# One over the deviation from Ln and Exp alone in an attention-with-norm kernel, with one activation table from the start and a new order of its first twelve blocks

## The chip, the cores and the metric

The kernel runs on one core of one Trainium2 chip. The core has five engines with queues of their own: TensorE (PE, with its weight loads shown apart as PEld), VectorE (DVE), ScalarE (ACT), GpSimd (POOL) and SyncE (SP, which here only issues DMAs). The metric is the device time of one execution in microseconds (us), taken as a median over several runs. The kernel before has a median of 792.28 us over 3 runs (791.06 to 794.29).

## The reference, cut to what matters

```python
x = A_x                                    # [1, 2048, 640] bf16
xn = (x - mean(x)) / sqrt(var(x) + 1e-5)   # per row of 640
# A: 32 heads of 192, the last 512 of 2048 cached keys and values
q = (xn @ wq).reshape(1, 2048, 32, 192).transpose(0, 2, 1, 3)
p = softmax(q @ k[:, :, -512:].T * 192 ** -0.5)
s = (p @ v[:, :, -512:]) -> [1, 2048, 6144] @ wo
# B: r = xn @ w_r; the two rows with the largest r get a gated MLP added
g = silu(B(xn))
out = x + s * g
```

What this case is about is the second line, and the order in which the first part of A is worked through.

## The kernel before, in words

Everything is one program for one core. The 2048 rows are 16 tiles of 128 (`n` = 0 to 15) in four quarters of four tiles (`t5` = 0 to 3). The 32 heads are 8 groups of 4, that is 2 pairs per group. A step `i` is one group, one quarter and one pair (64 steps); it has two blocks `b` (128 blocks in all), and each block two halves `a` of one row tile each. The order of every engine's queue is written out by hand: an instruction stands in its engine's queue where the Python emits it. The first 12 blocks (the head) come from the string `FIRST` (L618 to L636), whose tokens are worked off by `first` (L538); blocks 12 to 125 follow the fixed list `BLOCK` (L962); the last two follow `LAST`.

The tokens of the head that the change and the prediction speak of:

- `lx`, `lk`, `lq`, `x`, `k`, `v`, `wq`, `wo`: DMAs of x, keys, values and weights, most of them on SP's queue. `ko` orders the keys on POOL (L119), `kT` turns them by a DMA (L123), `kturn` turns the first pair's keys on PE.
- `bn.n.c` and `st.t5.i`: statistics of a row tile on DVE (L247 and L505, closed by L249 and L507). `sa` does the same for some tiles of the last quarter on ACT (L516, L520).
- `dev.n` (L252, ACT) and `app.n` (L255 and L256, DVE): deviation and normalisation of the four tiles of the first quarter. `nw.t5.i` (L217 to L240 and L188) is one over the deviation of the other quarters, in seven instructions per quarter, and `ap.n.e` (L181) their normalisation on the engine `e` (`a` ACT, `v` DVE, `g` POOL).
- `turn.n.e`: five PE transposes of a normalised tile (L274) and the copy into `xnT` on ACT or DVE (L275).
- `exp`: an explicit load of the activation table (L560).
- `q.i.c.e`: one third of the queries of a step (`q_whole`, L300, five matmuls; with a fourth number, for half of the rows) and their scaling into `qT` on DVE (L304) or ACT (L306). `qa` and `qb` are the same in two phases of half-height matmuls (L331, L341).
- `S.b.a`: scores of a half block (L358, six matmuls). `M.b.a`: its row maximum on DVE (L363). `E.b.a`: two exponentials on ACT (L370) and, with `.s` or at the second half, the DMA transpose of the result into `pT`.
- `P.b.e`: products with the values (L401), one over the sum on DVE (L408), and the scaling of the two halves on the two engines named: DVE (L412, one instruction) or ACT (L415, two instructions). `W.k`: products with `wo` (L443).

Scores live in two PSUM buffers (`ps_s`): `S` of a half block needs the `E` of the half block two places before it. Four smaller PSUM buffers (`ps_f`) serve `turn`, `q`, `P` and `W` in the head. `M` of a half block has to be done before its `E`. In this way PE, DVE and ACT pass each half block around, and each engine works strictly in the order of its queue.

Of the kernel before, what the change touches and what calls it, by code (L numbers as in the profile page):

```python
# [21 lines left out]
def kernel(ctx, tc, A_x, A_k_cache, A_v_cache, A_wq, A_wo, B_x, B_w_r, B_w_gate, B_w_up, B_w_down, out):  # L22
# [157 lines left out]

    def ln_apply(eng, n, src):  # L181
        if eng == "a":
            nc.scalar.activation(out=xn[:, n, :], in_=src, func=ACT.Identity, bias=nmr[:, n:n + 1], scale=rstd[:, n:n + 1])
# [4 lines left out]
    def ln_nmr(mean_ap, rstd_ap, nmr_ap):  # L188
        nc.vector.scalar_tensor_tensor(out=nmr_ap, in0=mean_ap, scalar=-1.0, in1=rstd_ap, op0=ALU.mult, op1=ALU.mult)
# [27 lines left out]
    def rsqrt_parts(var_ap, out_ap):  # L217

        T = {}

        def ln():
            T["v"] = small.tile([P, 4], FP32, name="nw_v")
            T["a"] = small.tile([P, 4], FP32, name="nw_a")
            nc.scalar.activation(out=T["a"], in_=var_ap, func=ACT.Ln, bias=eps_t[:, 0:1], scale=1.0)

        def ex():
            nc.scalar.activation(out=out_ap, in_=T["a"], func=ACT.Exp, scale=-0.5)

        def v():
            nc.gpsimd.tensor_scalar(out=T["v"], in0=var_ap, scalar1=EPS, scalar2=None, op0=ALU.add)  # L230

        def s1():
            nc.vector.scalar_tensor_tensor(out=T["a"], in0=out_ap, scalar=-0.5, in1=out_ap, op0=ALU.mult, op1=ALU.mult)

        def s2():
            nc.vector.tensor_tensor(out=T["a"], in0=T["a"], in1=T["v"], op=ALU.mult)

        def s3():
            nc.vector.scalar_tensor_tensor(out=out_ap, in0=T["a"], scalar=1.5, in1=out_ap, op0=ALU.add, op1=ALU.mult)
# [10 lines left out]

    def first_dev(n):
        nc.scalar.activation(out=rstd[:, n:n + 1], in_=mv[:, n, 1:2], func=ACT.Sqrt, bias=eps_t[:, 0:1], scale=1.0)  # L252

    def first_apply(n):
        nc.vector.reciprocal(out=rstd[:, n:n + 1], in_=rstd[:, n:n + 1])  # L255
        nc.vector.tensor_scalar(out=xn[:, n, :], in0=x_in[0][:, n, :], scalar1=mv[:, n, 0:1], scalar2=rstd[:, n:n + 1],  # L256
                                op0=ALU.subtract, op1=ALU.mult)
# [13 lines left out]
    def turn_tile(n, copy):  # L271
        tp = f_tile([P, DC, P], BF16, "tp")
        for dc in range(DC):
            nc.tensor.transpose(out=tp[:, dc, :], in_=xn[:, n, dc * P:(dc + 1) * P], identity=ident)  # L274
        copy(out=xnT[:, n], in_=tp)  # L275

# [84 lines left out]
    def row_max(b, a):  # L361
        nm_of[b, a] = small.tile([P, 2], FP32, name="nm")
        rm = nc.vector.tensor_reduce(out=nm_of[b, a], in_=s_of[b, a], axis=AX.X, op=ALU.max, negate=True)  # L363
# [690 lines left out]
```

## Time and profile before

| | before |
|---|---|
| median of 3 runs | 792.28 us |
| the profiled execution | 792.27 us |
| its span, first to last instruction | 790.3 us |
| TensorE's granted clock | 1.0 |
| busy: PE, DVE, ACT, POOL | 776.1, 580.0, 526.5, 339.6 us |
| the head (to the first matmul of block 12) | 84.06 us |

The times of the profile count from the span's start. The profiled execution lies 1.97 us above its span and 0.01 us from the median. A row of a group of instructions has the line of the kernel, the engine, the operation, what it writes and reads, how often it ran, its busy time, the mean of one in ns, and the idle time of the engine just before it with what ended that. The table of stretches has a row for each stretch of the span with the busy time of each engine in it. The chain of waits starts from the last instruction and goes back, at each step to what released it.

### The profile page before, as it was taken

The page shows a single profiled execution, that of the slowest core. Times are in us where ns is not written, and L with a number is a line of the kernel's source. Part 1 is how long each engine was busy: PE and PEld are TensorE (multiplying, and loading weights), DVE is VectorE, ACT ScalarE, POOL GpSimd, SP SyncE. Part 2 cuts the span into 40 slices and gives each one's busy share as a digit, 9 for nine tenths or more (in the row PEclk, how much of TensorE's full clock was granted, in tenths as well). Part 3 has the DMA queues.
Part 4 walks back from the last instruction along what each step waited for, and adds up shares of the span by engine and source line. Part 5 has one row for each costly group of instructions (what it writes and reads, how often), then busy time and mean ns, then how long its engine had stood idle before and what let it go on. Part 6 is the DMA issues. An engine that isn't in the chain of part 4 may idle for free.

```text
span 790.3 us, 27041 instructions
## 1 busy us (share of the span) xinstructions
PE 776.1 (98%) x11380; PEld 572.6 (72%) x11380; DVE 580.0 (73%) x1073; ACT 526.5 (67%) x950; POOL 339.6 (43%) x282
## 2 busy tenths in 40 slices
PE   8899999999999999999999999999999999999997
PEld 4457677777777777777777777777777777777775
DVE  7898788887787767667766766766766776776775
ACT  6676666677666677777666666766666666666661
POOL 1334110023110226626210102569986894266895
PEclk9999999999999999999999999999999999999999
DMA  9989999899999999999999999999999899999993
GB/s 240 196 170 174 174 184 170 146 193 163 175 187 188 211 176 192 191 170 201 175 200 183 194 218 183 158 191 188 165 176 179 149 187 168 182 179 169 181 177 93
DMA packets 447418, 142.18 MB, mean 180 GB/s; under 512 B 414724, under 2 KB 446726, under 8 KB 447296
## 3 DMA queue, kind: packets, MB, share of 16 engines
q1 hardware_dynamic: 437456, 130.84, 99.9%
q10 hardware_dynamic: 8816, 6.76, 3.2%
q0 software_dynamic: 1024, 2.85, 1.4%
q8 instruction: 89, 1.46, 0.8%
q14 instruction: 33, 0.27, 0.1%
HBM read 40.31 MB, written 2.63 MB: 54 GB/s over the span
## 4 chain that ended last, share of the span: by engine, by line
PE 90%; DVE 3%; DMA 3%; ACT 2%; issue 1%; POOL 1%; POOLq 0%; SPq 0%; DVEq 0%; ACTq 0%
PE w L443 25%; PE q_ps L331 24%; PE o_ps L401 20%; PE s L358 19%; DVE nm L363 1%; PE q_ps L300 1%; ACT pexp L370 1%; DMA pT<-pexp 1%; DMA v_sb<-in_A_v_cache_dram 1%; DMA out_dram<-fin_o 1%; DMA oT<-o_sb 0%; ACT xnT L275 0%; POOL fin_o L487 0%; DMA x_in<-in_A_x_dram 0%; PE tp L274 0%
## 5 line engine op out<-in xcount | busy, mean ns | idle before, releaser
L363 DVE TENSOR_REDUCE nm<-s 128x2 f32<-128x1024 f32 x256 | 313.0, 1223 | 137.7 <-PE s L358 135.8
L370 ACT ACTIVATE pexp<-s,nm 128x512 bf16<-128x512 f32 x512 | 324.1, 688 | 97.2 <-DVE nm L363 91.4
L331 PE MATMUL q_ps<-xnT,wq_g 64*128 64x512 bf16 (+1 forms) x2340 | 232.5, 323 | 0.0
L443 PE MATMUL w<-wo_g,oT 64*128 64x320 bf16 (+1 forms) x3096 | 231.4, 295 | 0.1
L358 PE MATMUL s<-kT,qT 64*128 64x512 bf16 x1536 | 211.5, 376 | 2.8 <-ACT pexp L370 2.6
L443 PEld LDWEIGHTS <-oT 64*128 64x128 bf16 x3096 | 170.1, 94 | 58.5 <-DMA oT<-o_sb 0.9
L401 PEld LDWEIGHTS <-pT 64*128 64x128 bf16 x4096 | 177.3, 94 | 31.4 <-issue 2.8
L401 PE MATMUL o_ps<-v_sb,pT 64*128 64x193 bf16 x4096 | 195.4, 243 | 2.9 <-DMA pT<-pexp 2.0
L415 ACT ACTIVATE o_sb<-o_ps,rl 128x192 bf16<-128x192 f32 x246 | 90.1, 418 | 128.8 <-DVE rl L408 128.5
L331 PEld LDWEIGHTS <-wq_g 64*128 64x128 bf16 x2340 | 125.7, 99 | 46.0 <-DVE qT L304 0.5
L149 POOL COPY wo_g<-wo_g 64x1920 bf16<-64x1920 bf16 x32 | 57.3, 1793 | 187.9 <-DMA wo_g<-in_A_wo_dram 165.5
L358 PEld LDWEIGHTS <-qT 64*128 64x128 bf16 x1536 | 84.7, 94 | 58.0 <-issue 3.8
L482 DVE TENSOR_TENSOR s_acc<-s_acc,w 128x320 f32<-128x320 f32 x192 | 85.0, 484 | 31.3 <-PE w L443 31.2
L343 ACT ACTIVATE qT<-q_ps 128x1024 bf16<-128x1024 f32 x114 | 92.4, 811 | 7.1 <-PE q_ps L331 1.0
L412 DVE TENSOR_TENSOR o_sb<-o_ps,rl 128x384 bf16<-128x384 f32 x133 | 74.1, 557 | 4.7
L119 POOL COPY k_perm<-k_raw 128x768 bf16<-128x768 bf16 x30 | 24.3, 826 | 94.1 <-DMA k_raw<-in_A_k_cache_dram 69.7
L893 POOL TENSOR_SCALAR yh<-y_bc,oh 128x640 f32<-128x640 f32 x32 | 60.3, 1884 | 4.7 <-DMA y_bc<-y_d 1.9
L894 POOL TENSOR_TENSOR xn<-xn,yh 128x640 bf16<-128x640 bf16 x32 | 45.0, 1406 | 2.7
L880 POOL TENSOR_TENSOR tz<-tz,xn 128x640 f32<-128x640 f32 x16 | 22.4, 1399 | 54.4 <-ACT tz L879 54.4
L408 DVE RECIPROCAL rl<-o_ps 128x2 f32<-128x2 f32 x256 | 30.7, 160 | 13.6 <-PE o_ps L401 8.9
L953 POOL TENSOR_TENSOR s_acc<-s_acc,x_fin 128x640 f32<-128x640 f32 x16 | 22.4, 1398 | 11.3 <-DMA x_fin<-in_A_x_dram 10.5
L881 POOL TENSOR_TENSOR xn<-tz,xn 128x640 bf16<-128x640 f32 x16 | 22.4, 1398 | 1.3
(140 smaller groups left out, 274.9 us busy)
## 6 DMA issues: line engine op xcount, KB each, us to landing
wo_g<-in_A_wo_dram SPq DMA_DIRECT2D x32, 240.0 KB, 4.1
k_raw<-in_A_k_cache_dram SPq DMA_DIRECT2D x32, 192.0 KB, 3.3
v_sb<-in_A_v_cache_dram SPq DMA_DIRECT2D x32, 192.0 KB, 3.8
wq_g<-in_A_wq_dram SPq DMA_DIRECT2D x14, 288.0 KB, 3.8
pT<-pexp SPq DMA_TRANSPOSE x246, 4.0
wq_g<-in_A_wq_dram SPq DMA_DIRECT2D x14, 192.0 KB, 3.4
x_fin<-in_A_x_dram SPq DMA_DIRECT2D x16, 160.0 KB, 3.8
oT<-o_sb SPq DMA_TRANSPOSE x126, 3.6
```

What stands on the lines that cost most here:

```text
L149: nc.gpsimd.tensor_copy(out=grp[g][("wo", pr)][half(1), cs, :], in_=grp[g][("wo", pr)][half(0), cs, :])
L331: mm = nc.tensor.matmul(q_ps[k][:, 0:n] if type(q_ps) is list else q_ps[:, k, 0:n], lhsT=wq[half(r), dc, c:2 * Dh:3], rhs=xnT[half(r), tok ...
L343: nc.scalar.activation(out=out, in_=q_ps[:, :, 0:n], func=ACT.Copy, scale=scale)
L358: nc.tensor.matmul(s_of[b, a][:, r, :], lhsT=qT_of[i][half(r), c, u * P:(u + 1) * P], rhs=grp[g][("kT", pr)][half(r), :, c, :], start=(c = ...
L363: rm = nc.vector.tensor_reduce(out=nm_of[b, a], in_=s_of[b, a], axis=AX.X, op=ALU.max, negate=True)
L370: nc.scalar.activation(out=p_ring[:, b % 2, a, :, hh, :].rearrange("p (x j) e -> p x j e", x=2), in_=s_of[b, a][:, hh, :].rearrange("p (j ...
L401: nc.tensor.matmul(o_of[b][r][:, a, 0:Dh + 1], lhsT=pT_ring[half(r), b % RP, a, k, :], rhs=v_ring[half(r), (g * PAIRS + pr) % RV, k, 0:Dh ...
L412: nc.vector.tensor_tensor(out=o_sb, in0=src, in1=rl[:, r].unsqueeze(2).unsqueeze(3).to_broadcast([P, 2, 3, HK]), op=ALU.mult)
L415: nc.scalar.activation(out=o_sb[:, a], in_=src[:, a], func=ACT.Copy, scale=rl[:, r, a:a + 1])
L443: nc.tensor.matmul(w_ps[r][:, 0:cs.stop - cs.start], lhsT=oT_ring[half(r), bs[pr] % RT, c, :], rhs=grp[g][("wo", pr)][half(r), c, cs], sta ...
L482: nc.vector.tensor_tensor(out=acc, in0=acc, in1=src, op=ALU.add)
L893: nc.gpsimd.tensor_scalar(out=yh, in0=M["y_bc"][:, j, :], scalar1=M["oh"][:, n, j:j + 1], scalar2=None, op0=ALU.mult)
```

## The change

One over the deviation is now made by the same two ACT instructions for all tiles: `Ln` of the variance plus epsilon, then `Exp` with a scale of -0.5 (`ln_rstd`). In the first quarter they stand for the `Sqrt` on ACT and the reciprocal on DVE; in the other quarters, where `Ln` and `Exp` were there already, the three instructions of the Newton step on DVE, the added epsilon on POOL and the shifted mean `nmr` on DVE are gone. The normalisation is now (x - mean) * rstd everywhere (`ln_rows`), no longer x * rstd + nmr. The explicit load of the table that has both functions stands on ACT's queue right after its two first DMA issues, ahead of all work, and no other table is loaded in the head. The string `FIRST` has a new order, in which some instructions also change their engine. A new token `tt.n` (`turn_pair`) turns two row tiles at once by twenty transposes of half height, which end in two copies. `q_phase` and the scaling are made more general; what they emit for the tokens used is as before. The two gathered rows of part B lose their shifted mean in the same way; their own Newton steps stay.

```diff
-    def ln_apply(eng, n, src):
-        if eng == "a":
-            nc.scalar.activation(out=xn[:, n, :], in_=src, func=ACT.Identity, bias=nmr[:, n:n + 1], scale=rstd[:, n:n + 1])
-            return
-        (nc.gpsimd if eng == "g" else nc.vector).tensor_scalar(
-            out=xn[:, n, :], in0=src, scalar1=rstd[:, n:n + 1], scalar2=nmr[:, n:n + 1], op0=ALU.mult, op1=ALU.add)
-
-    def ln_nmr(mean_ap, rstd_ap, nmr_ap):
-        nc.vector.scalar_tensor_tensor(out=nmr_ap, in0=mean_ap, scalar=-1.0, in1=rstd_ap, op0=ALU.mult, op1=ALU.mult)
+    def ln_rstd(out, var):
+        t = small.tile([P, 4], FP32, name="ln_v")[:, 0:out.shape[-1]]
+        nc.scalar.activation(out=t, in_=var, func=ACT.Ln, bias=eps_t[:, 0:1], scale=1.0)
+        nc.scalar.activation(out=out, in_=t, func=ACT.Exp, scale=-0.5)
+
+    def ln_rows(eng, out, src, mean, r):
+        (nc.gpsimd if eng == "g" else nc.vector).tensor_scalar(out=out, in0=src, scalar1=mean, scalar2=r, op0=ALU.subtract, op1=ALU.mult)
+
+    def ln_apply(eng, n, src):
+        ln_rows(eng, xn[:, n, :], src, mv[:, n, 0:1], rstd[:, n:n + 1])
...
-    def rsqrt_parts(var_ap, out_ap):
...
-        return [ln, ex, v, s1, s2, s3]
...
+    def first_apply(n):
+        ln_apply("v", n, x_in[0][:, n, :])
+
     def first_dev(n):
-        nc.scalar.activation(out=rstd[:, n:n + 1], in_=mv[:, n, 1:2], func=ACT.Sqrt, bias=eps_t[:, 0:1], scale=1.0)
-
-    def first_apply(n):
-        nc.vector.reciprocal(out=rstd[:, n:n + 1], in_=rstd[:, n:n + 1])
-        nc.vector.tensor_scalar(out=xn[:, n, :], in0=x_in[0][:, n, :], scalar1=mv[:, n, 0:1], scalar2=rstd[:, n:n + 1],
-                                op0=ALU.subtract, op1=ALU.mult)
+        ln_rstd(rstd[:, n:n + 1], mv[:, n, 1:2])
...
+    def turn_pair(n, es):
+        tp = [f_tile([P, 2, DC, P // 2], BF16, "tp") for _ in range(2)]
+        for u in range(2):
+            for dc in range(DC):
+                for r in range(2):
+                    nc.tensor.transpose(out=tp[r][:, u, dc, :], in_=xn[half(r), n + u, dc * P:(dc + 1) * P], identity=ident[half(r), half(r)])
+        for r in range(2):
+            copies[es[r]](out=xnT[:, n:n + 2, :, half(r)], in_=tp[r])
...
     FIRST = """
-    lx.0.s lx.1.a lk.0.s lk.1.s lq.0.a lx.2.s lx.3.s v.0 x.1.0 bn.0.0 bn.1.0 x.1.1 bn.1.1 dev.1 bn.0.1 app.1 dev.0 k.1.0 app.0 bn.2.0 turn.0.a bn.3.0 bn.3.1 turn.1.a v.1 kturn.av bn.2.1 wq.1 dev.3 q.0.2.0.a k.1.1 q.0.0.0.v dev.2 v.2 q.0.1.0.a
-    ko.1 app.2 app.3 st.1.0
-    S.0.0 M.0.0 exp x.2 turn.2.a turn.3.a S.0.1 kT.1 M.0.1 st.1.1 E.0.0.s st.1.2 wo.0 q.0.1.1.a q.0.0.1.a q.0.2.1.v E.0.1
-    S.1.0 wo.1 st.1.3 st.1.4 S.1.1 M.1.0 st.1.5 E.1.0.s q.1.1.a M.1.1 q.1.2.a E.1.1 st.1.6 q.1.0.v st.1.7 nw.1.0
-    S.2.0 nw.1.1 nw.1.2 M.2.0 wo.2 S.2.1 nw.1.3 nw.1.4 nw.1.5 M.2.1 nw.1.6 st.2.0 E.2.0.s ap.7.g ap.6.v P.0.vv E.2.1
-    S.3.0 M.3.0 ap.4.a v.3 S.3.1 turn.6.a ap.5.g wd.0 turn.5.a turn.4.v turn.7.v E.3.0.s st.2.1 st.2.2 P.1.va M.3.1 wo.3 st.2.3 E.3.1 q.2.1.a q.2.2.v st.2.4 wd.1 q.2.0.v P.2.va
-    S.4.0 M.4.0 S.4.1 E.4.0 x.3 M.4.1 st.2.5 q.3.1.a E.4.1 wd.2 st.2.6 st.2.7 nw.2.0 q.3.2.a nw.2.1 nw.2.2
-    S.5.0 M.5.0 nw.2.3 E.5.0 nw.2.4 q.3.0.v S.5.1 wd.3 nw.2.5 sa.3.0.0 nw.2.6 M.5.1 E.5.1 sa.3.2.0 W.0.v ap.10.g
-    S.6.0 ap.11.g M.6.0 gk.0 E.6.0 ap.9.g ap.8.v W.1.v P.3.av S.6.1 M.6.1 P.4.va
-    S.7.0 st.3.6 E.6.1 turn.10.v turn.11.v turn.9.a turn.8.v sa.3.0.1 M.7.0 S.7.1 E.7.0 gk.1 q.4.2.v gq.0 q.4.1.v q.4.0.a
-    qa.5.0.1 sa.3.1.0
-    S.8.0 M.7.1 go.0 E.7.1 st.3.7 gw.0 sa.3.2.1 sa.3.1.1 nw.3.0 nw.3.1 M.8.0 W.2.v qb.5.0.1 nw.3.2 nw.3.3 nw.3.4 nw.3.5 P.5.av S.8.1 M.8.1 gq.1 nw.3.6 E.8.0 E.8.1 P.6.va ap.15.v
-    qa.5.2 ap.12.v
-    S.9.0 S.9.1 M.9.0 ap.14.g turn.12.v turn.14.v E.9.0 ap.13.g qb.5.2 turn.13.v M.9.1 turn.15.v
-    S.10.0 gT.0 E.9.1 gk.2 gk.3 P.7.vv W.3.v M.10.0 E.10.0 S.10.1 gv.0 P.8.vv W.4.a
-    qa.6.0.1 M.10.1 gd.0
-    S.11.0 E.10.1 M.11.0 B.11 go.1 E.11.0 W.5.v qb.6.0.1 P.9.av q.6.2.v S.11.1 M.11.1 E.11.1 gw.1 gv.1
+    lx.0.s lx.1.a lk.0.s lk.1.s lq.0.a exp lx.2.s lx.3.s v.0 x.1.0 bn.1.0 bn.0.0 bn.1.1 x.1.1 bn.0.1 dev.1 dev.0 wq.1 app.1 app.0 bn.2.0 turn.1.a turn.0.a k.1.0 bn.3.0 k.1.1 kturn.av ko.1 v.1 v.2 bn.3.1 bn.2.1 q.0.2.0.a dev.3 dev.2 q.0.0.0.v app.2 st.1.0 app.3 q.0.1.0.a x.2 kT.1
+    S.0.0 M.0.0 turn.2.a turn.3.a st.1.1 S.0.1 E.0.0.s q.0.1.1.a M.0.1 q.0.0.1.a q.0.2.1.a E.0.1
+    S.1.0 st.1.2 q.1.2.a st.1.3 S.1.1 st.1.4 M.1.0 E.1.0 M.1.1 st.1.5 wo.0 wo.1 E.1.1 q.1.1.a wo.2 st.1.6 q.1.0.v st.1.7
+    S.2.0 M.2.0 S.2.1 nw.1.0 st.2.0 E.2.0.s M.2.1 ap.6.v P.0.va S.3.0 M.3.0 ap.7.g wd.0 v.3 ap.4.v E.2.1 tt.6.va
+    S.3.1 ap.5.g turn.5.a E.3.0.s turn.4.v st.2.1 st.2.2 P.1.av st.2.3 M.3.1 q.2.2.a q.2.1.v E.3.1 q.2.0.v st.2.4 wo.3 P.2.va
+    S.4.0 S.4.1 M.4.0 wd.1 E.4.0 x.3 M.4.1 E.4.1 q.3.1.a st.2.5 st.2.6 wd.2 q.3.2.a S.5.0 M.5.0 E.5.0.s q.3.0.v st.2.7
+    S.5.1 M.5.1 nw.2.0 wd.3 sa.3.0.0 E.5.1 W.0.v ap.11.g S.6.0 M.6.0 P.3.va ap.9.g ap.10.g sa.3.2.0
+    S.6.1 M.6.1 ap.8.v W.1.v E.6.0 P.4.va E.6.1 gk.0 gk.1 st.3.6 S.7.0 turn.9.v turn.11.v turn.8.a turn.10.v M.7.0
+    S.7.1 q.4.0.a gq.0 M.7.1 gw.0 E.7.0 sa.3.0.1 gq.1 q.4.1.a q.4.2.v sa.3.1.0 st.3.7 qa.5.0.1
+    S.8.0 E.7.1 sa.3.1.1 sa.3.2.1 nw.3.0 go.0 M.8.0 W.2.v qb.5.0.1 P.5.av S.8.1 M.8.1 E.8.0.s E.8.1 P.6.va qa.5.2 ap.14.g ap.12.v
+    S.9.0 S.9.1 ap.15.g M.9.0 ap.13.g turn.14.v turn.12.v E.9.0.s qb.5.2 M.9.1 gT.0 gv.0 turn.13.v turn.15.a
+    S.10.0 M.10.0 gk.2 P.7.va W.3.v E.9.1 E.10.0 W.4.a P.8.vv S.10.1 gk.3 qa.6.0.1 go.1 M.10.1
+    S.11.0 M.11.0 gd.0 E.10.1 W.5.v qb.6.0.1 E.11.0 P.9.va B.11 q.6.2.a S.11.1 M.11.1 E.11.1 gv.1 gw.1
     """.split()
...
-            M["rs2"] = M["s"].tile([2, 2], FP32, name="rs2")
+            M["rs2"] = M["s"].tile([2, 1], FP32, name="rs2")
...
-            ln_nmr(mv2[:, 0:1], rs2[:, 0:1], rs2[:, 1:2])
-            nc.vector.tensor_scalar(out=M["xsel"][0:2, :], in0=M["xg"], scalar1=rs2[:, 0:1], scalar2=rs2[:, 1:2], op0=ALU.mult, op1=ALU.add)
+            ln_rows("v", M["xsel"][0:2, :], M["xg"], mv2[:, 0:1], rs2)
```

More of the change, by code (lines that the diff above doesn't have):

```diff
@@ L215, in rsqrt_newton @@
         return [one, two, three] + [s1, s2, s3] * 3
-    def rsqrt_parts(var_ap, out_ap):
[L219 to L239, printed above, removed]
-        return [ln, ex, v, s1, s2, s3]
     st0 = {}
@@ L340, in q_phase @@
                 for k in range(2):
-                    nc.scalar.activation(out=out[:, k], in_=q_ps[k][:, 0:n], func=ACT.Copy, scale=scale)
+                    q_scale(es[k], out[:, k], q_ps[k][:, 0:n])
             else:
-                nc.scalar.activation(out=out, in_=q_ps[:, :, 0:n], func=ACT.Copy, scale=scale)
+                q_scale("a", out, q_ps[:, :, 0:n])
     s_of = {}
```

44 lines of the change are left out of this document (28 added, 16 removed).

## The prediction, made before the changed kernel ran

> **What bounds the kernel now.** I read the page first, then the chain of waits, then a table of stretches cut where the chain changes hands.
>
> ```profile
> span 790.3 us, 27041 instructions
> PE 90%; DVE 3%; DMA 3%; ACT 2%; issue 1%; POOL 1%; POOLq 0%; SPq 0%; DVEq 0%; ACTq 0%
> ```
>
> ```profile
> 10.60:23.00 12.40, 10.78 (x83) 5.21 (x84) 11.20 (x23) 9.74 (x19) 1.89 (x3) 1.00 1.12 234
> 23.00:36.10 13.10, 10.78 (x142) 6.91 (x140) 11.67 (x27) 8.28 (x14) 7.02 (x5) 1.00 1.07 188
> 36.10:52.70 16.60, 16.13 (x198) 9.89 (x194) 15.95 (x34) 12.36 (x27) 5.38 (x9) 1.00 0.82 170
> 52.70:66.10 13.40, 13.28 (x159) 8.17 (x160) 10.35 (x23) 11.28 (x25) 3.96 (x10) 1.00 0.96 160
> 66.10:84.06 17.96, 17.93 (x253) 12.95 (x252) 13.62 (x26) 10.00 (x20) 6.61 (x13) 1.00 1.06 180
> 84.06:780.00 695.94, 694.10 (x10416) 521.13 (x10416) 505.50 (x908) 469.40 (x838) 308.40 (x230) 1.00 1.07 180
> ```
>
> Behind the stretch's bounds and its length stand the busy us of PE, PEld, DVE, ACT and POOL, then PE's granted clock and the DMA share. From 84.06 on, PE is busy 694.10 of 695.94 us and the other engines have room. The same holds from 66.10. The change leaves that work as it is, apart from two tiny instructions of part B. So the time is 84.06, the end of the head, plus a rest of 792.27 - 84.06 = 708.2 us that I hold fixed. A microsecond gained or lost in the head is one in the result if it is still there at 66.1. All that PE does not work between 10.6 and 66.1 is 1.62 + 2.32 + 0.47 + 0.12 = 4.5 us. Its rows also stretch where it is fed late, so a little more can be had.
>
> ```profile
> 11.05 1.28 ACT L560
> 12.34 1.29 ACT xnT L275 x2
> ...
> 30.55 4.30 DMA v_sb<-in_A_v_cache_dram
> ...
> 42.26 1.16 DVE nw_a L233
> ...
> 52.67 0.82 PE s L358 x6
> 53.50 3.35 PE q_ps L300 x15
> ...
> 63.70 1.08 ACT pexp L370 x2
> ...
> 66.07 0.82 PE s L358 x6
> ```
>
> These are pieces of the chain, start, length, engine and line. Before 52.67 it runs mostly through DVE and ACT, at 52.67 it passes to PE, from 63.70 to 66.03 to ACT once more, and from 66.07 it is PE alone. The change touches three of these pieces by name: the table load, a Newton instruction (L233), and the late load of the values, which in the new order stands ahead of the DMA transpose of E.2.1.
>
> **The change part by part.** The durations are means of the same forms, over the head:
>
> ```profile
> L370 ACT ACTIVATE pexp<-s,nm 128x512 bf16<-128x512 f32 x46 | 29.1, 688 | 12.6 <-DVE nm L363 9.3 <-PE o_ps L401 3.2
> L401 PE MATMUL o_ps<-v_sb,pT 64*128 64x193 bf16 x320 | 16.0, 243 | 1.2 <-DVE xnT L275 0.6 <-DMA v_sb<-in_A_v_cache_dram 0.4 <-DMA pT<-pexp 0.2
> L412 DVE TENSOR_TENSOR o_sb<-o_ps,rl 128x384 bf16<-128x384 f32 x13 | 7.2, 557 | 0.5
> L274 PE MATMUL tp<-ident,xn 128*128 128x128 bf16 x80 | 5.6, 220 | 1.1 <-DVE xn L256 1.1
> L415 ACT ACTIVATE o_sb<-o_ps,rl 128x192 bf16<-128x192 f32 x14 | 5.1, 419 | 4.4 <-DVE rl L408 4.4
> L306 ACT ACTIVATE qT<-q_ps 128x512 bf16<-128x512 f32 x6 | 3.5, 601 | 1.5 <-PE q_ps L300 1.5
> L520 ACT ACTIVATE xn<-x_in,sums 128x640 bf16<-128x640 bf16 x3 | 2.5, 841 | 0.0
> L256 DVE TENSOR_SCALAR xn<-x_in,mv,rstd 128x640 bf16<-128x640 bf16 x4 | 1.8, 446 | 0.1
> L252 ACT ACTIVATE rstd<-mv,eps_t 128x1 f32<-128x1 f32 x4 | 1.2, 300 | 3.0 <-DVE mv L249 2.7 <-DVE rstd L255 0.3
> L183 ACT ACTIVATE xn<-x_in,nmr,rstd 128x640 bf16<-128x640 bf16 x1 | 0.9, 917 | 0.0
> L224 ACT ACTIVATE nw_a<-mv,eps_t 128x4 f32<-128x4 f32 x3 | 0.9, 305 | 1.0 <-DVE mv L507 0.6 <-POOL mv L521 0.3
> L227 ACT ACTIVATE rstd<-nw_a 128x4 f32<-128x4 f32 x3 | 0.6, 213 | 0.1
> L255 DVE RECIPROCAL rstd<-rstd 128x1 f32<-128x1 f32 x4 | 0.6, 146 | 0.1
> L236 DVE TENSOR_TENSOR nw_a<-nw_a,nw_v 128x4 f32<-128x4 f32 x3 | 0.5, 163 | 0.3
> L189 DVE SCALAR_TENSOR_TENSOR nmr<-mv,rstd 128x4 f32<-128x4 f32 x3 | 0.5, 154 | 0.0
> ```
>
> The first four tiles: Sqrt (0.300) becomes Ln and Exp (0.305 + 0.213), 0.22 us more per tile on ACT; the reciprocal (0.146) leaves DVE. Tiles 0 and 1 lose nothing, since DVE has the other tile's statistics to do meanwhile. For tiles 2 and 3 all four ACT instructions stand in a row ahead of the scaling of a query third, so the last normalisation comes up to 2 x 0.22 = 0.44 later.
>
> The table: the Sqrt table's load at the start is replaced one for one, and the one at 11.05 goes. What it held up are the copies at 12.34. But those need transposes that ran only just then:
>
> ```profile
> 11.62 0.73 PE L274 MATMUL tp<-ident,xn 128*128 128x128 bf16 x10
> ```
>
> Five of these ten are done about 0.37 after their start, at 12.0. So of the 1.28 us at most 0.34 lay on the path, the rest beside these transposes. With 0.44 against it, the bounds to 23.0 are a gain of 0.34 and a loss of 0.44, and I take nothing.
>
> The Trainium skill, "ScalarE: Activation LUTs", section "What ACT_TABLE_LOAD costs", gives a switch as about 1.28 us of load and 1.38 us of drain. By that the removal would free 2.66 us of ACT, and if all of the drain counted the time would be 1.4 us less than mine. The trace agrees on the load and shows no drain: the load ends at 12.33 and the copy starts at 12.34.
>
> The Newton step and the shifted mean: four DVE instructions per quarter, two of them at 0.163 and 0.154 and two of the same size and kind, 4 x 0.158 = 0.63 us. From 23.0 to 36.1 DVE loses this and half of P.0's scaling (0.557), and gains ap.4 (0.446; the new subtract form is the one of L256): 0.74 less on an engine busy 11.67 of 13.10. ACT gains two scalings (0.84) and loses ap.4 (0.917). On the other side, P.0's scalings now stand on ACT ahead of E.2.1, which has to free the buffer for S.3.1. That makes S.3.1 about a microsecond late, but its row maximum was queued on DVE until long after it:
>
> ```profile
> 26.70 0.82 PE L358 MATMUL s<-kT,qT 64*128 64x512 bf16 x6 [0.84 <-ACT pexp L370]
> ...
> 31.76 1.21 DVE L363 TENSOR_REDUCE nm<-s 128x2 f32<-128x1024 f32 x1
> ```
>
> S.3.1 ended at 27.52 and waited 4.2 us for DVE, which hides it. Bounds here: 0.74 and the 0.4 that PE waited for the values, 1.1 gained, to 0.84 lost if the scaling on ACT holds the exponentials after all. DVE is the busier engine, so I take 0.5 gained. The paired transposes of tiles 6 and 7 are not in the trace: 20 at 16.0/320 = 0.05 (the half-height products with the values) are 1.0 us, against 10 x 0.07 = 0.7 before, with 0.35 (two side by side) and 1.4 (each at the full price) as bounds; PE has 2.3 us free here, so this costs nothing, and up to 0.7 if it had none.
>
> From 36.1 to 52.7 DVE is busy 15.95 of 16.60 and loses 0.63 again, and the chain had 1.16 us at a Newton instruction. Bounds: nothing gained, 1.16 gained. DVE is the engine on the path, so I take 0.8.
>
> From 52.7 to 66.1 the gain is partly handed back on ACT. The next two score products that matter, S.9.0 and S.9.1, need E.8.0 and E.8.1, and ACT does its queue in order. From the first third of q.4 on it now holds: two scalings of q.4 (1.2; one before), four pairs of exponentials (4 x 29.1/23 = 5.1), three squares at 0.84, an identity sum, which I price alike, and four reads of sums at some 0.1 where the next instruction does not cover them (3.8), Ln and Exp (0.5), the scaling of qb (two like q.4's, 1.2) and of P.5 (0.84): 12.6 us. It starts about 1.8 after S.7.1 (0.65 of scores and a third of 3.35): 14.4 against 66.07 - 52.67 = 13.4. Bounds: 1.0 lost, nothing lost (PE hides it); I take 0.7 lost, nearer to the sum, because this stretch of the chain was ACT's already at its end.
>
> From 66.1 on P.7's second half, a copy and a third of q.6 go to ACT, which is busy 10.00 of 17.96. P.7's scaling and E.9.1 (0.84 + 1.27) are hidden by W.3, W.4 and P.8 on PE, all ahead of S.10.1 that needs E.9.1; without them it would cost these 2.1. DMAs: the second weights of the queries go ahead of the keys of the second pair, the other loads of the first rows behind, all still ahead of the keys' transpose, so it starts with the same bytes done. The next group's keys go behind block 6's transpose; its scores start at block 16, four blocks of 695.94/116 = 6.0 us after the head. POOL, under half busy everywhere but 23.0 to 36.1, loses one small instruction per quarter. All this at zero.
>
> Sum: 0 - 0.5 - 0.8 + 0.7 + 0 = -0.6; 792.27 - 0.6 = 791.7 us. The profiled execution is within 0.01 us of the median, so the same holds for that.
>
> **The rivals.** *DVE was the whole trouble (faster).* With DVE relieved and the order fitted to it, PE runs through from 10.6 on. For it: the chain is DVE's before 52.67, and PE's free time there is 4.4 us. Against it: in the first stretch nothing is taken from DVE but two reciprocals and a scaling, and PE cannot be fed before the tiles are normalised. All 4.5 us gone and nothing handed back gives 787.8.
>
> *ACT becomes the bound of the head (slower).* At four places something new stands on ACT between a row maximum and its exponentials: P.0 ahead of E.2.1 (0.84), q.2.2 beside P.1 ahead of E.3.1 (0.60 + 0.84), P.3 and a sum ahead of E.6.0 (0.84 + 0.84), q.4.1 and a sum ahead of E.7.1 (0.60 + 0.84). Together 5.4 us, and 796.2 at least when PE has used up 1.5 us of its cover: 792.27 + 5.4 - 1.5. It decides where these exponentials end later than the PE work queued ahead of the scores that need their buffer. For it: 52.7 to 66.1 is ACT's already. Against it: ACT is busy only 63% from 23.0 to 36.1 and 74% after.
>
> *The change does not do what it says*, because another load is put between Ln or Exp and a Copy, Identity or Square. Three quarters at 1.28 us would be 3.8 more, 795.5. Against it: before, the same mix ran after 12.33 with no further load.
>
> **How the numbers follow.** My forecast has 0.58, DVE 0.24, ACT 0.15, the extra load 0.03. The likeliest is 791.7. The low end takes in the faster rival with the bounds of the first two stretches, 787.0. The high end goes just past the slower rival's start, 796.5; its rest and the rest of the faster one are left out. About 0.5%, 4 us, is what a measurement of this kernel can tell from no change. Faster by more than that is the DVE rival, 0.24, slower is the ACT rival, 0.15, and the forecast and the extra load lie within, 0.61.
>
> **What would show it.** One table load, near 1.7, and none at 11; the copies of tiles 2 and 3 still near 12 to 13.5. S.7.1 near 51.5 instead of 52.67, S.9.1 near 65.5 instead of 66.07, block 12 near 83.5. ACT without idle time from the first third of q.4 to E.8.1. I am wrong if block 12 starts before 80 or after 88, or if the rest after it is not 708.2.

## The result, and the profile after

| | before | after |
|---|---|---|
| median of four runs each | 791.67 us (791.01 to 794.29) | 796.05 us (795.84 to 797.15) |
| ratio after / before, 95% interval | | 1.0054 (1.0032 to 1.0077) |
| profiled execution | 792.27 us | 796.09 us |
| its span; mean granted clock | 790.3 us; 1.0 | 794.3 us; 0.995 |
| block 12 starts (first matmul, L331 before, L325 after) | 84.06 | 89.89 |
| rest, from there to the end of the execution | 708.2 us | 706.2 us |

The changed kernel is 4.4 us slower by the medians, 3.8 us by the two profiled executions. The head lost 5.83 us, of which the rest gave 2.0 back. On the page of after POOL has come into the chain that ended last, where it had 1% before:

```profile
span 794.3 us, 27055 instructions
PE 90%; POOL 4%; ACT 2%; DMA 2%; issue 1%; DVE 1%; SPq 0%; POOLq 0%; ACTq 0%; DVEq 0%
```

The table of stretches of after, cut where it was cut before, with two finer ones behind it and the part after the head last (columns: busy us of PE, PEld, DVE, ACT, POOL, then granted clock, DMA share and GB/s):

```profile
10.60:23.00 12.40, 11.26 (x94) 5.59 (x94) 11.10 (x20) 8.85 (x19) 2.40 (x3) 1.00 1.15 236
23.00:36.10 13.10, 9.51 (x103) 5.89 (x98) 9.11 (x20) 6.88 (x14) 9.59 (x5) 0.74 0.96 177
36.10:52.70 16.60, 16.60 (x207) 10.01 (x206) 14.47 (x27) 11.53 (x25) 7.03 (x5) 1.00 0.84 162
52.70:66.10 13.40, 12.17 (x133) 6.92 (x131) 8.30 (x17) 10.37 (x24) 5.47 (x11) 1.00 0.90 173
66.10:84.06 17.96, 15.23 (x237) 10.99 (x234) 12.14 (x24) 10.06 (x23) 8.62 (x5) 1.00 0.83 142
...
30.00:32.00 2.00, 2.00 (x26) 1.70 (x25) 1.37 (x4) 1.86 (x3) 2.00 (x2) 0.50 1.09 209
32.00:34.00 2.00, 2.00 (x18) 1.10 (x15) 0.76 (x4) 0.51 (x2) 0.82 (x1) 0.50 0.60 103
...
92.00:780.00 688.00, 687.10 (x10322) 519.46 (x10319) 501.73 (x899) 466.95 (x836) 305.17 (x230) 1.00 1.08 181
```

From 10.6 to 84.06 PE does not work for 1.14 + 3.59 + 0 + 1.23 + 2.73 = 8.7 us; it was 4.6 before. The new idle time lies at 23 to 36.1 and after 52.7, and there ACT is no fuller than before by more than 0.06 us and DVE is emptier. POOL is busier in all five stretches. Besides, the clock is 0.50 from 30 to 34, which no stretch of before shows. The groups by form name the instruction, first after, then before:

```profile
L187 POOL TENSOR_SCALAR xn<-x_in,mv,rstd 128x640 bf16<-128x640 bf16 x8 | 20.2, 2534 | 7.9 <-ACT rstd L184 7.8
```

```profile
L185 POOL TENSOR_SCALAR xn<-x_in,rstd,nmr 128x640 bf16<-128x640 bf16 x7 | 6.4, 921 | 6.4 <-DVE nmr L189 6.4
```

The same normalisation of a row tile on POOL takes 2.53 us as (x - mean) * rstd and took 0.92 as x * rstd + nmr. Eight of them are 20.2 us of the head. The chain of waits of after shows where they are on the path:

```profile
22.25 1.85 POOL xn L187
...
24.82 1.83 POOL wo_g L149
26.76 2.50 POOL xn L187
...
47.86 7.50 POOL xn L187 x3
...
66.21 7.70 POOL xn L187 x3
```

There are three places: tiles 7 and 5 with a copy of `wo` between them, tiles 11, 9 and 10 in a row, tiles 14, 15 and 13 in a row. PE's own waits and timeline in after say what stood behind them:

```profile
PE tp L248 <- POOL xn L187: 5.2, 3, 2.6
PE s L353 <- ACT pexp L365: 2.3, 3, 1.5
```

```profile
1.66 1.28 ACT L557 ACT_TABLE_LOAD   x1 [1.66 <-PEq L1032]
...
11.98 1.29 ACT L249 COPY xnT<-tp 128x640 bf16<-128x640 bf16 x2 [1.08 <-PE tp L248]
...
25.13 0.47 PE L257 MATMUL tp<-ident,xn 64*128 64x64 bf16 x20
27.06 0.82 PE L353 MATMUL s<-kT,qT 64*128 64x512 bf16 x6 [1.46 <-ACT pexp L365]
29.31 1.25 PE L248 MATMUL tp<-ident,xn 128*128 128x128 bf16 x10 [1.42 <-POOL xn L187]
30.49 2.77 PE L396 MATMUL o_ps<-v_sb,pT 64*128 64x193 bf16 x32
...
73.96 0.73 PE L248 MATMUL tp<-ident,xn 128*128 128x128 bf16 x10 [2.57 <-POOL xn L187]
```

The brackets give the idle time of the engine ahead of a row and what ended it. Transposes (L248) waited for POOL at 29.31 and 73.96. At 27.06 S.3.1 waited 1.46 us for ACT. After these idle times the 32 products of P.1 take 2.77 us, where 31 of them took 1.49 in the timeline of before (its second row is S.4.0, which is used further down):

```profile
29.49 1.49 PE L401 MATMUL o_ps<-v_sb,pT 64*128 64x193 bf16 x31 [0.56 <-DVE xnT L275]
...
36.16 1.53 PE L358 MATMUL s<-kT,qT 64*128 64x512 bf16 x12
```

So there are two suspects, POOL's new form and the clock after S.3.1's wait, and two parts of the change that might do either: the arithmetic and the order.

### The profile page after: what moved, and what is told of

Its sections match the earlier page's. It is cut to its first block, busy times and chain, and to the rows that moved or that the text cites. A ratio compares the mean times of both kernels' runs of the same rounds, so it can differ in the third digit from the quotient of the medians.

```text
span 794.3 us, 27055 instructions
## 1 busy us (share of the span) xinstructions
PE 777.7 (98%) x11390; PEld 575.3 (72%) x11390; DVE 574.9 (72%) x1050; ACT 527.3 (66%) x960; POOL 352.1 (44%) x280
## 3 DMA queue, kind: packets, MB, share of 16 engines
q8 instruction: 89, 1.46, 0.8%
## 4 chain that ended last, share of the span: by engine, by line
PE 90%; POOL 4%; ACT 2%; DMA 2%; issue 1%; DVE 1%; SPq 0%; POOLq 0%; ACTq 0%; DVEq 0%
PE w L438 24%; PE q_ps L325 24%; PE o_ps L396 20%; PE s L353 19%; POOL xn L187 2%; PE q_ps L284 2%; ACT pexp L365 1%; DMA pT<-pexp 1%; DMA x_in<-in_A_x_dram 1%; POOL fin_o L482 0%; PE tp L248 0%; POOL fin_o L463 0%; DMA k_raw<-in_A_k_cache_dram 0%; PE gu_ps L797 0%; POOL wo_g L149 0%
## 5 line engine op out<-in xcount | busy, mean ns | idle before, releaser
L325 PE MATMUL q_ps<-xnT,wq_g 64*128 64x512 bf16 (+1 forms) x2340 | 232.7, 323 | 0.1
L325 PEld LDWEIGHTS <-wq_g 64*128 64x128 bf16 x2340 | 126.2, 100 | 45.8 <-issue 0.8
L303 ACT ACTIVATE qT<-q_ps 128x1024 bf16<-128x1024 f32 (+2 forms) x120 | 95.1, 795 | 8.0 <-PE q_ps L325 1.6
L187 POOL TENSOR_SCALAR xn<-x_in,mv,rstd 128x640 bf16<-128x640 bf16 x8 | 20.2, 2534 | 7.9 <-ACT rstd L184 7.8
```

What stands on the lines that cost most here:

```text
L303: nc.scalar.activation(out=out, in_=in_, func=ACT.Copy, scale=scale)
```

## The experiments

All start from the changed kernel unless it is said otherwise. A ratio is to the kernel before, on the same chip, with its 95% interval; starts of block 12 are from the profiled execution. Single executions differ already ahead of the edits: S.2.0, the first scores of block 2, starts before POOL's first tile, at 20.98 in the changed kernel and between 20.86 and 21.81 in the versions made from it, whose edits all act later. So where a small difference matters it is also given counted from S.2.0.

**The changed kernel with POOL in the old form.** The shifted mean is made by one small instruction on POOL itself.

```diff
+        if eng == "g":
+            nc.gpsimd.tensor_scalar(out=nmr[:, n:n + 1], in0=mv[:, n, 0:1], scalar1=rstd[:, n:n + 1], scalar2=-1.0, op0=ALU.mult, op1=ALU.mult)
+            nc.gpsimd.tensor_scalar(out=xn[:, n, :], in0=src, scalar1=rstd[:, n:n + 1], scalar2=nmr[:, n:n + 1], op0=ALU.mult, op1=ALU.add)
+            return
```

> The changed kernel, with one edit: on POOL alone the normalisation is x * rstd + nmr again, with nmr made on POOL just ahead by a 128x1 instruction. Theory 1 (POOL's form: subtract then multiply takes 2.51 us where multiply then add took 0.92): the eight instructions are near 0.92 again, PE's 5.2 us of waiting for them go, granted clock 1.00 from 23 to 36 us, block 12 starts near 83.5 instead of 89.9, and the time is 789.5 to 792. Theory 2 (the new order itself costs, POOL only shows it): block 12 still starts after 87 and the time stays above 794. Theory 3 (the form matters but the new order had something to lose besides): 792 to 794.

Measured: 792.74 us (12 runs), ratio 1.0002 (0.9988 to 1.0016), block 12 at 84.34. The groups and the stretch from 23 us of this kernel:

```profile
L194 POOL TENSOR_SCALAR xn<-x_in,rstd,nmr 128x640 bf16<-128x640 bf16 x8 | 7.0, 870 | 0.8
L193 POOL TENSOR_SCALAR nmr<-mv,rstd 128x1 f32<-128x1 f32 x8 | 2.2, 279 | 7.1 <-ACT rstd L184 7.0
```

```profile
23.00:36.10 13.10, 10.42 (x125) 6.74 (x121) 9.69 (x22) 8.01 (x15) 7.26 (x6) 0.87 1.17 192
```

With the form alone put back the loss is gone: 89.89 - 84.34 = 5.55 us at block 12, and 5.78 counted from S.2.0. The clock still falls here, if less (0.87 against 0.74), so a fall comes without the new form too, and with it this kernel is no slower than the one before. PE's timeline shows S.3.1's wait and the slow P.1 again:

```profile
27.30 0.82 PE L359 MATMUL s<-kT,qT 64*128 64x512 bf16 x6 [1.46 <-ACT pexp L371]
...
29.70 2.70 PE L402 MATMUL o_ps<-v_sb,pT 64*128 64x193 bf16 x32
```

**The kernel before with POOL in the new form**, everything else as it was:

```diff
-        (nc.gpsimd if eng == "g" else nc.vector).tensor_scalar(
+        if eng == "g":
+            nc.gpsimd.tensor_scalar(out=xn[:, n, :], in0=src, scalar1=mv[:, n, 0:1], scalar2=rstd[:, n:n + 1], op0=ALU.subtract, op1=ALU.mult)
+            return
+        nc.vector.tensor_scalar(
```

> The kernel before, with one edit: POOL's seven normalisations of the head take the form (x - mean) * rstd. Theory 1: each goes from 0.92 to about 2.5 us, 11 us more on POOL; the old order has two of them ahead of the turns of tiles 5 and 7 and three ahead of those of 9 to 11, so PE waits some 3 to 6 us and the time is 795 to 798. Theory 2 (the order alone): POOL is under half busy in the old order, so the time stays within 1 us of before, 791 to 793.

Measured: 799.75 us (5 runs), ratio 1.0100 (1.0082 to 1.0119), block 12 at 90.31, 6.25 later than before. Its group by form and PE's wait:

```profile
L186 POOL TENSOR_SCALAR xn<-x_in,mv,rstd 128x640 bf16<-128x640 bf16 x7 | 17.5, 2507 | 2.9 <-DVE rstd L242 2.9
```

```profile
PE tp L277 <- POOL xn L186: 5.4, 3, 2.0
```

The form makes the loss in either order and with either arithmetic: taken out of the one kernel it gives the time back, put into the other it costs a little more than in the new order.

**The kernel before with the rest of the new arithmetic**: Ln and Exp for the first tiles, one early table load, no Newton step; old order, POOL in the old form.

```diff
-        return [ln, ex, v, s1, s2, s3]
+        return [ln, ex, none, none, none, none]
...
-        nc.scalar.activation(out=rstd[:, n:n + 1], in_=mv[:, n, 1:2], func=ACT.Sqrt, bias=eps_t[:, 0:1], scale=1.0)
+        nc.scalar.activation(out=t, in_=mv[:, n, 1:2], func=ACT.Ln, bias=eps_t[:, 0:1], scale=1.0)
+        nc.scalar.activation(out=rstd[:, n:n + 1], in_=t, func=ACT.Exp, scale=-0.5)
```

> The kernel before in its old order, with the new arithmetic except on POOL: Ln and Exp for the first four tiles, one table load at the start, no Newton step; the shifted mean and the old form of the normalisation stay. My prediction's terms: nothing from the table, up to 1.9 us less on DVE, of which some 0.5 to 1.2 reach the end: 790.5 to 791.5 against 791.7 to 792.3 before. Rival (the arithmetic was worth more than I saw, through the table load): under 790. Rival (Ln and Exp in front cost more than the load): over 792.5.

Measured: 792.66 us (12 runs), ratio 1.0002 (0.9987 to 1.0016), block 12 at 83.48, granted clock 1.00 through the head. The arithmetic without POOL's form gains 0.58 us at block 12 in this execution, 0.23 of it ahead of S.2.0 (21.29 against 21.52), and nothing that the medians can show. The 0.5 to 1.2 us expected of it did not come.

**The forms alone**, four of each in a row on one loaded tile; this kernel leaves out all of the reference's computation.

```diff
+    for _ in range(N):
+        g.tensor_scalar(out=y, in0=src, scalar1=r[:, 0:1], scalar2=m[:, 0:1], op0=ALU.mult, op1=ALU.add)
+    for _ in range(N):
+        g.tensor_scalar(out=y, in0=src, scalar1=m[:, 0:1], scalar2=r[:, 0:1], op0=ALU.subtract, op1=ALU.mult)
+    for _ in range(N):
+        g.tensor_scalar(out=y, in0=src, scalar1=m[:, 0:1], scalar2=r[:, 0:1], op0=ALU.add, op1=ALU.mult)
...
```

> A small kernel that computes nothing of the reference: thirteen forms of POOL's scalar instruction, four in a row of each, on 128x640 (two on 128x320), with nothing beside them, and two forms on DVE. Theory A (the pair multiply then add is quick, every other pair slow): subtract-multiply, add-multiply and multiply-subtract all take about 2.5 us, multiply-add 0.87 to 0.92. Theory B (subtract is slow as such): subtract alone and multiply-subtract are slow too, add-multiply is quick. Theory C (two operands read from memory in the slow path): immediates bring subtract-multiply down to about 0.9. DVE takes 0.43 to 0.45 in both forms. The half width takes about half if the cost is per element.

The groups by form. L50 subtracts and multiplies, L54 multiplies and subtracts, L62 is L50 with constants, L58 is a multiplication alone (a subtraction, L56, and an addition, L60, take the same 1.88 us), L48 multiplies and adds, L52 adds and multiplies; L75 and L77 are L50 and L48 on DVE:

```profile
L54 POOL TENSOR_SCALAR y<-src,r,m 128x640 bf16<-128x640 bf16 x4 | 10.0, 2501 | 0.4
L50 POOL TENSOR_SCALAR y<-src,m,r 128x640 bf16<-128x640 bf16 x4 | 10.0, 2495 | 0.0
...
L62 POOL TENSOR_SCALAR y<-src 128x640 bf16<-128x640 bf16 x4 | 9.4, 2351 | 0.3
L58 POOL TENSOR_SCALAR y<-src,r 128x640 bf16<-128x640 bf16 x4 | 7.5, 1883 | 0.4
...
L48 POOL TENSOR_SCALAR y<-src,r,m 128x640 bf16<-128x640 bf16 x4 | 3.7, 924 | 2.8 <-DMA src<-in_A_x_dram 2.8
L52 POOL TENSOR_SCALAR y<-src,m,r 128x640 bf16<-128x640 bf16 x4 | 3.5, 873 | 0.3
...
L77 DVE TENSOR_SCALAR y<-src,r,m 128x640 bf16<-128x640 bf16 x4 | 1.8, 447 | 0.1
L75 DVE TENSOR_SCALAR y<-src,m,r 128x640 bf16<-128x640 bf16 x4 | 1.8, 446 | 0.1
```

The 2.5 us belong to the form and not to the surroundings. A pair of an add and a multiplication is quick in either order, a pair with a subtraction is 2.7 times slower, and a single operation, even a multiplication, is slow too (1.88). DVE takes the same time for the two forms that it was given.

**Filling PE's idle time.** If the clock's fall were a second cost of the changed kernel, keeping PE busy would give it back: six matmuls of 128x512 whose result nobody reads, behind the paired transposes, and six more ahead of the transposes of tile 5.

```diff
+        elif op == "fill":
+            fill_ps = f_tile([P, W], FP32, "warm_ps")
+            for _ in range(n[0]):
+                nc.tensor.matmul(fill_ps, lhsT=idle[:, 0:P], rhs=idle, start=True, stop=True)
...
-    S.2.0 ... E.2.1 tt.6.va
-    S.3.1 ap.5.g turn.5.a
+    S.2.0 ... E.2.1 tt.6.va fill.6
+    S.3.1 ap.5.g fill.6 turn.5.a
```

> The changed kernel with six dummy matmuls (128x512, results unused) on PE behind the paired transposes of tiles 6 and 7 and six ahead of the turn of tile 5, where PE sat idle 1.46 and 1.42 us before the granted clock fell to a mean of 0.74 between 23 and 36 us. If the fall of the clock costs of its own: clock 1.00 there, P.1 takes 1.5 instead of 2.77 us and q.2 3.42 instead of 4.47, block 12 starts up to 2.3 us earlier and the time falls from 796.05 to 793.7 to 795. If POOL's instructions hold the end anyway: the clock is 1.00, but block 12 still starts at 89 to 90 and the time stays at 795.5 to 796.5.

Measured: 795.87 us (6 runs), ratio 1.0041 (1.0027 to 1.0054), block 12 at 89.48. The clock was 1.00 from 23 to 36.1 (and 0.90 from 66.1 to 84.06), and yet only 0.4 us came back: PE still waited 4.0 us for POOL's tiles, the longest 2.6. While POOL sets the end, the clock costs little here.

**The same filling with POOL in the old form** (the first experiment with `fill.6` behind `tt.6.va` only):

> The first experiment (POOL in its old form, new order) with six dummy matmuls on PE behind the paired transposes of tiles 6 and 7, where PE sat idle 1.46 us and the clock then fell to 0.5 for some 3 us. If that fall is what the new order still pays: clock 1.00 from 23 to 36 us, P.1 takes 1.5 instead of 2.7 us, block 12 starts at 82.7 to 83.5 instead of 84.34, the time is 0.8 to 1.6 us less than that of the first experiment. If DVE and ACT hold the next stretch anyway: block 12 stays at 84 to 84.5 and the time the same.

Measured: 789.86 us (6 runs), ratio 0.9965 (0.9951 to 0.9978), block 12 at 83.18. Two stretches of this kernel:

```profile
23.00:36.10 13.10, 11.05 (x145) 6.63 (x143) 12.18 (x24) 8.18 (x15) 6.87 (x6) 1.00 0.94 177
...
92.00:780.00 688.00, 687.77 (x10340) 519.96 (x10336) 500.63 (x902) 464.03 (x830) 309.88 (x232) 1.00 1.08 180
```

With POOL out of the way the clock counts: it is 1.00 in place of 0.87, P.1 takes 1.51 us in place of 2.70, and block 12 is 1.16 us earlier than without the filling (0.81 counted from S.2.0), six dummy matmuls included. More of the gain lies behind the head: from 92 to 780 PE is idle 0.23 us here, and 3.00 in the profiled execution of the first experiment:

```profile
92.00:780.00 688.00, 685.00 (x10292) 517.12 (x10291) 498.48 (x894) 465.72 (x831) 306.66 (x228) 1.00 1.08 180
```

There it waited once 1.8 us for the DMA transpose of part B's gathered rows and, in two waits, 1.2 us for `pT`.

**The new form on tiles 5 and 7 only**, the old one on POOL's other six:

```diff
-        if eng == "g":
+        if eng == "g" and n > 7:
```

> The first experiment with POOL's new form left on tiles 5 and 7 alone (two instructions of eight). If each late group costs on its own: PE waits 1.4 us for tile 5 and the clock falls for longer than in the first experiment, block 12 starts 2 to 3 us later, at 86.4 to 87.4, and the time is 794 to 795.5. If the head takes it up by 66 us (POOL's three instructions of the last quarter are what sets the end): block 12 at 84.3 to 85 and the time within 0.7 us of the first experiment.

Measured: 792.61 us (11 runs), ratio 1.0000 (0.9987 to 1.0012), block 12 at 86.33. Block 12 is 86.33 - 84.34 = 2.0 us later than in the first experiment, but 0.6 of it stands there at S.2.0 already (21.81 against 21.21). That leaves 1.4 us for the first two tiles, and 4.4 of the 5.78 for the six later ones. The medians do not show the 1.4: this profiled execution's rest was 706.9, the first experiment's 708.9.

**The filled kernel with an added negative mean**, (x + (-mean)) * rstd, with -mean from one small instruction:

```diff
-            nc.gpsimd.tensor_scalar(out=nmr[:, n:n + 1], in0=mv[:, n, 0:1], scalar1=rstd[:, n:n + 1], scalar2=-1.0, op0=ALU.mult, op1=ALU.mult)
-            nc.gpsimd.tensor_scalar(out=xn[:, n, :], in0=src, scalar1=rstd[:, n:n + 1], scalar2=nmr[:, n:n + 1], op0=ALU.mult, op1=ALU.add)
+            nc.gpsimd.tensor_scalar(out=nmr[:, n:n + 1], in0=mv[:, n, 0:1], scalar1=-1.0, scalar2=None, op0=ALU.mult)
+            nc.gpsimd.tensor_scalar(out=xn[:, n, :], in0=src, scalar1=nmr[:, n:n + 1], scalar2=rstd[:, n:n + 1], op0=ALU.add, op1=ALU.mult)
```

> The filled version (the sixth experiment) with POOL's normalisation as (x + (-mean)) * rstd, the negated mean made by a 128x1 instruction on POOL. If the quick pairs are those of add and multiply in either order, as the forms alone showed: each instruction takes 0.87 to 0.93 us in place too, block 12 starts at 82.9 to 83.5 and the time is within 0.1% of the filled version, 789 to 790.5. If what is quick alone is slow beside DVE's work: 2.5 us each, block 12 after 87 and the time over 793.

Measured: 788.90 us (5 runs), ratio 0.9960 (0.9945 to 0.9975), block 12 at 84.11. Its group by form:

```profile
L194 POOL TENSOR_SCALAR xn<-x_in,nmr,rstd 128x640 bf16<-128x640 bf16 x8 | 7.2, 898 | 1.1 <-POOL nmr L193 0.4
```

Subtracting by adding is 0.90 us. Block 12 came later than the 82.9 to 83.5 expected: against the filled version (the sixth experiment) 0.49 us are there at S.2.0 already (21.35 against 20.86), and 0.44 come when a normalisation on DVE takes 2.03 us in place of 1.58 (see the last section). By their ratios this version and the filled one are about 3 us faster than the kernel before and about 7 faster than the changed one; between the two there is nothing to choose.

**P.0's scaling all on DVE**, without filling, POOL in the old form:

```diff
-    ... M.2.1 ap.6.v P.0.va S.3.0 ...
+    ... M.2.1 ap.6.v P.0.vv S.3.0 ...
```

> The first experiment (POOL in its old form, new order, no dummy matmuls) with both halves of P.0 scaled on DVE, as in the old order. If ACT's scaling ahead of E.2.1 is what leaves PE idle 1.46 us and lets the clock fall: E.2.1 starts right after its row maximum, at about 25.0 instead of 25.98, PE's wait for S.3.1 falls to 0.5 us or less, the clock stays at 1.00 from 23 to 36 us, and block 12 starts at 83.0 to 83.8 instead of 84.34. If DVE's 0.56 us more hands it on: the clock is 1.00, and block 12 stays at 84.1 to 84.8.

Measured: 791.02 us (12 runs), ratio 0.9989 (0.9978 to 1.0000), block 12 at 83.02, clock 1.00 from 23 to 36.1. PE's timeline there:

```profile
26.02 0.47 PE L263 MATMUL tp<-ident,xn 64*128 64x64 bf16 x20 [0.77 <-DVE xn L187]
26.33 0.81 PE L359 MATMUL s<-kT,qT 64*128 64x512 bf16 x6
...
29.20 0.45 PE L254 MATMUL tp<-ident,xn 128*128 128x128 bf16 x5 [1.57 <-DVE xn L187]
29.59 1.51 PE L402 MATMUL o_ps<-v_sb,pT 64*128 64x193 bf16 x32
...
35.72 1.46 PE L359 MATMUL s<-kT,qT 64*128 64x512 bf16 x12
...
51.56 0.82 PE L359 MATMUL s<-kT,qT 64*128 64x512 bf16 x6 [0.32 <-ACT pexp L371]
...
65.00 0.82 PE L359 MATMUL s<-kT,qT 64*128 64x512 bf16 x6 [0.15 <-ACT pexp L371]
```

S.3.1 starts at 26.33 without a wait; in the first experiment it started at 27.30 behind 1.46 us of idle time. So P.0's scaling on ACT, ahead of E.2.1, made S.3.1 late. Block 12 is 84.34 - 83.02 = 1.3 us earlier, 1.0 counted from S.2.0. But P.1 starts hardly earlier, at 29.59 against 29.70, because here PE waits 1.57 us for DVE's normalisation of tile 4. What is gained is P.1's pace, 1.51 us in place of 2.70, and so the clock. That S.3.1's wait is what made it fall is not shown: here a longer wait left it at 1.00.

**Both of these together**, P.0 on DVE and the six dummy matmuls:

> e9 (products' scaling of block 0 on DVE, POOL in the old form) with the six dummy matmuls of e6 behind the paired transposes. In e9 the granted clock is 1.00 in the head and block 12 starts at 83.02, yet its ratio is 0.9989 against 0.9965 of e6, whose block 12 starts at 83.18. Theory A: the dummy matmuls are worth only the clock they keep up, so here they are worth nothing: ratio 0.998 to 1.000, PE idle from 92 to 780 near the 1.8 us of e9, block 12 at 83.0 to 83.2. Theory B: what e6 gained beyond the head comes from the dummy matmuls shifting the work against the DMAs: ratio near 0.9965, PE idle from 92 to 780 near the 0.2 us of e6, block 12 again at 83.0 to 83.4.

Measured: 790.66 us (11 runs), ratio 0.9990 (0.9978 to 1.0001), block 12 at 84.79, PE idle 688.00 - 686.45 = 1.55 us from 92 to 780. The ratio and the idle time are A's, but neither theory had what the profile shows, a clock that fell all the same:

```profile
26.23 0.47 PE L263 MATMUL tp<-ident,xn 64*128 64x64 bf16 x20 [1.00 <-DVE xn L187]
26.90 2.66 PE L563 MATMUL warm_ps<-idle 128*128 128x512 bf16 x6 [0.20 <-DVE o_sb L413]
```

```profile
23.00:36.10 13.10, 11.19 (x113) 5.44 (x107) 11.17 (x22) 7.01 (x13) 6.91 (x6) 0.87 0.97 173
```

The dummy matmuls themselves ran at half clock here, 2.66 us for six, and S.3.1 stood behind them. So this profiled execution can't decide between A and B for a kernel whose clock stays up, and why the two faster versions have a shorter rest stays open. The rest moves with PE's waits in it (705.5 to 709.0 us over the profiled executions; in all but one with a wait there, the longest is for a DMA), and what sets those was not tried.

## Why the prediction was wrong

- **That the head decides, with the rest fixed.** The head decided: its end moved by 5.83 us. The rest was not fixed. It was 706.2 in place of "708.2 us that I hold fixed"; from 92 to 780 PE is idle 0.90 us after and, by the row below, 1.84 before, the longest of it a wait for `pT`. That term was off by 2.0 us and hid a third of the loss.

```profile
92.00:780.00 688.00, 686.16 (x10311) 515.97 (x10306) 499.30 (x898) 464.76 (x831) 308.40 (x230) 1.00 1.08 180
```

- **First tiles and table, 0.** Right in kind: one load, at 1.66, none at 11, and the copies at 11.98. S.2.0 starts 0.54 us earlier than before (20.98 against 21.52), but the other executions of the new order have it from 20.86 to 21.81. Of the 0.58 us that the arithmetic alone gained at block 12, 0.23 are from here.
- **23.0 to 36.1, "I take 0.5 gained".** Wrong. S.3.1 came about as late as said, 27.06 against 26.70 although the work ahead of it was 0.5 us early (S.2.1 ended at 22.45, before at 22.99), and DVE did hide that from its row maximum. But PE had nothing to do meanwhile: it stood 1.46 us, and later ran at half clock, which nothing in the sum stood for. The step looked for the one who waits for S.3.1 and not at PE, which can't go past it. From the start of S.2.0 to that of S.4.0 it is 36.16 - 21.52 = 14.6 us before, 15.8 in the first experiment and 14.8 with P.0 on DVE. So with POOL in its old form 1.2 and 0.2 us are lost where 0.5 gained was forecast; the difference of the two is about that of P.1's pace. The paired transposes, estimated at 1.0 us, took 0.47.
- **36.1 to 66.1, 0.8 gained and 0.7 handed back.** The profile of after can't show it, since POOL's tiles hold that stretch. With them quick, in the first experiment and with P.0 on DVE alike, it is 15.84 us from S.4.0 to S.7.1 in place of 52.67 - 36.16 = 16.51, so 0.7 gained, near the 0.8, and then 13.45 and 13.44 us to S.9.1 in place of 13.40, so next to nothing handed back: the 0.7 on ACT was not there. With P.0 on DVE, S.7.1, S.9.1 and block 12 start at 51.56, 65.00 and 83.02, near the forecast's 51.5, 65.5 and 83.5, but in part by luck: the errors of the terms around the 0.8 nearly cancel, and P.0 is not on the engine that the forecast had it on. In the first experiment, which differs from the changed kernel in POOL's form alone, they start at 52.87, 66.32 and 84.34, so that execution has none of the 0.6 us either.
- **The step that failed:** "POOL, under half busy everywhere but 23.0 to 36.1, loses one small instruction per quarter." and with it "All this at zero". The new form was priced for DVE ("the new subtract form is the one of L256") and not for POOL, whose row in the trace, 0.92 us, was of the other form. On POOL it takes 2.53, with eight tiles 20.2 - 6.4 = 13.8 us more in the head, one tile of it new. Busy shares could not say that this is harmless: the tiles come three in a row, 7.5 us, and PE's transposes need the last of them. The trace of before has no normalisation of that form on that engine, and so its cost should have been bounded from both sides like the paired transposes, instead of being passed over. The term was put at nothing and is worth 5.8 us at the end of the head.
- **The rivals.** ACT as the bound of the head has the right time, 796.2, by coincidence: ACT is busy 10.37 of 13.40 us from 52.7 to 66.1, less than before. Of its four places the first, P.0 ahead of E.2.1, did make PE wait. The range held 796.05 only because it went just past this rival's start, which is the same coincidence. There was no further table load in the head. That DVE was the whole trouble fell too: DVE has 9.11 us in place of 11.67 from 23 to 36.1, and PE was idle for longer. "I am wrong if block 12 starts before 80 or after 88": it started at 89.89. The rival that was missing is POOL.

## What to carry to other kernels

When a formula is rewritten for several engines, price the new form on each of them, and measure alone what the trace does not have: here the form that costs DVE the same costs POOL 2.7 times as much. An engine that is half idle is still on the path where its work comes in a row ahead of something that the bound engine needs, so look at the longest row and not at the share. When an instruction of the bound engine gets later, ask what that engine does meanwhile, even if whoever uses its result has time.

## What the runs showed of the hardware that I had not expected

*POOL's forms.* For 128x640: 0.87 to 0.92 us for a pair of add and multiplication, 2.50 with a subtraction in it, 1.88 for any single operation tried; DVE takes 0.45 for the two forms that it was given. The Trainium skill, "GPSIMD Engine Reference", section "Key points", says that for elementwise work DVE is structurally about 2 times faster. The quick pairs agree (924/447 = 2.1); the pairs with a subtraction do not (2495/446 = 5.6), and single operations were not run on DVE here.

*The clock.* It fell to 0.50 although no idle time of PE between 24 and 30 was longer than 1.46 us, and stayed there for 4 us or more in the changed kernel. Neither the longest idle piece nor the sum of the pieces says when it falls: pieces of 0.71, 1.46 and 0.51 us (first experiment) and of 0.71, 1.00 and 0.20 (P.0 on DVE, filled) were followed by a fall, pieces of 0.71, 1.35 and 0.38 (the added negative mean) and of 0.70, 0.77 and 1.57 (P.0 on DVE) were not. What decides it stays open. The mean clock of one kernel also differs from run to run, and the time with it: of the 12 runs of the first experiment the six with a mean clock of 0.997 or less took 793.22 to 795.28 us, the six with 0.998 or more 790.02 to 792.27. The Trainium skill, "TensorE: Matmul & The Clock Gate", section "What's actually happening", has the half clock follow at least one idle window of about 3.4 us, free-running so that its place varies. A place that varies would fit these runs; an idle window of that length was not there.

*DVE beside POOL.* In the kernel with P.0 on DVE one normalisation on DVE took 1.45 us in place of 0.45, while POOL was copying `wo`. The timeline of DVE and POOL:

```profile
24.52 1.45 DVE L187 TENSOR_SCALAR xn<-x_in,mv,rstd 128x640 bf16<-128x640 bf16 x1
...
24.01 1.78 POOL L149 COPY wo_g<-wo_g 64x1920 bf16<-64x1920 bf16 x1 [0.59 <-DMA wo_g<-in_A_wo_dram]
```

It ended at 25.97, 0.18 us after the copy. The same instruction took 1.58 us in the filled kernel and 2.03 with the added negative mean, and ended 0.17 and 0.18 us after the copy there. In the first experiment the copy started at 25.33, after this normalisation had ended, and it took 0.44 us. So it is the copy beside it that held it. The paired transposes waited for this normalisation, 0.77 to 1.35 us in these three versions and not at all in the first experiment.
